# Two small products placed ahead of the last block of scores, and another engine that waits for the output

## The chip, the cores and the metric

The kernel runs on one core of one Trainium2 chip. The core has five engines with their own instruction streams: TensorE (PE, matrix products), VectorE (DVE), ScalarE (ACT), GpSimd (POOL) and SyncE (SP), which here issues nearly all transfers from device memory (HBM). The transfers are carried by 16 DMA engines. The engines meet only at semaphores. The metric is the device time of one execution in microseconds (us); less is better.

## The reference

One decode step of two blocks on the same input x (2 batches, 1 position, 1024 features), mixed by a gate. Only the parts that matter here:

```python
g = _sigmoid((x * gate_w).sum(-1, keepdims=True))
# a: attention with a cache, 32 heads of 128, 16384 cached positions, 2 batches
q = (x @ wq) by head
p = softmax(einsum("bhqd,bhkd->bhqk", q, k_cache) * 128 ** -0.5)
a = einsum("bhqk,bhkd->bhqd", p, v_cache) as rows @ wo
# b: a mixer and an MLP
h  = gelu(layernorm(x) @ w1)           # then shifted by +-1 and +-2 positions
x1 = x + shifted(h) @ w2               # one position only, so shifted(h) is zero
b  = x1 + gelu(layernorm(x1) @ w3) @ w4
return g * a + (1 - g) * b
```

All arrays are bf16. The two caches hold 268 MB each; with the weights 572.5 MB are read, once.

## The kernel before, in words

The attention is cut into 32 units: 16 pairs of heads times 2 batches (s = 0 and 1). A unit reads 8 MB of K and 8 MB of V. For a unit, SP loads K into one of two cells of SBUF (cell 0 for s = 0, cell 1 for s = 1). DVE turns it in 8 pieces into one of two buffers kt (L631, a transpose of 128 x 2048 words each), and PE computes the scores of a piece from it with 8 matmuls (L652, `pe_scores`). So there are 8 blocks of scores, and DVE's piece n waits for PE's block n - 2. After block 8, DVE transposes the scores (st, L636) and takes the maximum (m, L640); ACT makes a diagonal from it (Dm, L668), PE spreads it (R, L661), DVE takes the bound (nb, L688), ACT does the exponentials in two halves (L674), PE sums (tot, L697), and DVE takes the reciprocal (rinv, L693). The product with V (L702) follows in the unit's next turn, since the loop loads V of turn i - 1 in turn i. V has one cell, number 3.

The same cell 3 holds at first the big weights, one after the other: wq, then w3 (7 MB), then w4 (7 MB), then the first V. `linear` (L500) computes a row product such as x @ w3 with many small matmuls on PE (L510): 64 of 448 columns for w3, into the banks `oacc`, and 112 of 256 columns for w4, into the bank `ot`. `Line` (L21) notes which engine read and wrote what, and puts in the waits; `ln.dma` issues a load on SP after those who used the cell.

The first two units (s = 0, 1 of pair 0) are written out ahead of the loop by `first_unit` (L790). Around them the program text gives the order on each engine:

- SP: loads of wq, w1, w2, K of unit 0, then (when wq's product is done) w3, then K of unit 1 (L808, after DVE's piece 4 of unit 0), then w4 (L813, issued through L82, after w3's product), then the loop.
- PE: unit 0's 8 blocks, R and tot; then w3's product; then unit 1's 8 blocks, R and tot; then w4's product. Only then PE raises `pvd1` and `wod` (L828, L829).
- DVE: unit 0's pieces and softmax steps; then the transpose of w3's result (L816) and, together with ACT, the gelu that ends with h2T (L496); then unit 1's; then the rows `brow` (L834).

In the loop (L847, turns 1 to 15) SP waits and loads in this order: K for s = 0 (after DVE's piece 4 of s = 1 of the turn before), V of the turn before for s = 0 (L856, waits on `pvd1`), a piece of wo (L859, waits on `wod`), then K for s = 1 and V for s = 1. For the first turn `pvd1` is the increment of L828, so the first V waits for w4's product, because it overwrites w4's cell.

At the end, the two rows of the output go out from SP and ACT (L955), and SP waits for both landings (L959, L960), then all engines meet at the closing barrier.

Of the kernel before, what the change touches and what calls it, by code (L numbers as in the profile page):

```python
# [88 lines left out]
def kernel(  # L89
# [17 lines left out]
    B, Sq, D = A_x.shape  # L107
    _, H, Sk, Dh = A_k_cache.shape
    F = B_w3.shape[1]
    assert Sq == 1 and B == 2 and Dh == P and P == 128  # L110
    KC = D // P
    FC = F // P
# [6 lines left out]
    NCK = NJ // CT  # L119
# [13 lines left out]
    def sb(shape, dtype, name):  # L133
        return const.tile(shape, dtype, name=name)
# [3 lines left out]
    def S(name):  # L138
        if name not in sems:
            sems[name] = tc.alloc_semaphore(name)  # L140
        return sems[name]
# [5 lines left out]
    st = sb([P, GT, QP], FP32, "st")  # L147
# [26 lines left out]
    xn2T = sb([P, KC, B], BF16, "xn2T")  # L174
    h2T = sb([P, FC, B], BF16, "h2T")
# [19 lines left out]
    oacc = [oacc2[:, k, :] for k in range(2)]  # L195
# [4 lines left out]
    ot_ps = psum.tile([P, NQ], FP32, name="ot")  # L200

    def region(cell, elements):
        return mem[:, cell * CELL : cell * CELL + elements]
# [21 lines left out]
    def wait(engine, name, value):  # L225
        if isinstance(value, int) and value == 0:
            return
        engine.wait_ge(S(name), value)
# [7 lines left out]
    with tc.tile_critical(no_gpsimd_drain=True):  # L236
        PE, DVE, ACT, POOL, SP = nc.tensor, nc.vector, nc.scalar, nc.gpsimd, nc.sync
# [94 lines left out]
        def many(count, make, reads, writes):  # L332

            ln.wait("PE", ln.needs(reads, writes))
            for n in range(count):
                ins = make(n)
            stamp = ln._stamp(ins, "PE")
            ln.note(stamp, reads, writes)
            return stamp
# [160 lines left out]
        def linear(actT, w, R, N, act_key, w_key, banks, out_keys):  # L500

            G = N // Q4
            width = G // len(banks)
            jobs = [
                (r, g, k) for r in range(R) for k in range(len(banks)) for g in range(Q4)
            ]

            def one(n):
                r, g, k = jobs[n]
                return PE.matmul(  # L510
                    banks[k][QP * g : QP * g + B, 0:width],
                    lhsT=actT[:, r, :],
                    rhs=w[:, r, g * G + k * width : g * G + (k + 1) * width],
                    start=(r == 0),
                    stop=(r == R - 1),
                    skip_group_check=True,
                )

            return many(len(jobs), one, [act_key, w_key], out_keys)
# [85 lines left out]
        def chunk_ids(s):  # L605
            low, high = list(range(NCK // 2)), list(range(NCK // 2, NCK))
            return high + low if K_CELL[s] == 0 else low + high
# [4 lines left out]
        def pool_unit(i, s, hi):  # L612
            wait(POOL, f"sc{s}7", i)
            dst = qw[s][:, :, NG - 1 : NG - 1 + QP * (Q4 - 1) + 1 : QP]
            row = qd[:, i, s, :] if isinstance(i, int) else qd[:, bass.ds(i, 1), s, :].rearrange("p o v -> p (o v)")
            POOL.tensor_tensor(  # L616
                out=dst,
                in0=row.unsqueeze(2).to_broadcast([P, 4, Q4]),
                in1=mask4[:].unsqueeze(1).to_broadcast([P, 4, Q4]),
                op=ALU.mult,  # L620
            ).then_inc(S(f"qwd{s}"), 1)

        def dve_scores(i, s, hi, hi16):
            for n, c in enumerate(chunk_ids(s)):
                if n == 0:
                    wait(DVE, f"kl{s}", hi16)
                if n >= 2:
                    wait(DVE, f"sc{s}{n - 2}", hi)
                else:
                    wait(DVE, f"sc{1 - s}{n + 6}", hi if s else i)  # L630
                DVE.transpose(  # L631
                    out=kt[n % 2][:],
                    in_=k_view(s)[:, c * CT : (c + 1) * CT, :].rearrange("p j d -> p (j d)").bitcast(FP32),
                ).then_inc(S(f"tr{s}{n}"), 1)
            wait(DVE, f"sc{s}7", hi)
            DVE.transpose(  # L636
                out=st[:].rearrange("p j r -> p (j r)"), in_=sps[s][:]
            ).then_inc(S(f"stT{s}"), 1)
            wait(DVE, f"stT{s}", hi)
            DVE.tensor_reduce(out=m_t[:], in_=st[:, :, 0:NG], axis=AX.XY, op=ALU.max).then_inc(S(f"mx{s}"), 1)  # L640

        def pe_scores(i, s, hi):
            wait(PE, f"qwd{s}", hi)
            wait(PE, f"stT{s}", i)
            for n, c in enumerate(chunk_ids(s)):
                wait(PE, f"tr{s}{n}", hi)
                ktb = kt[n % 2][:].bitcast(BF16).rearrange("p (j w k e) -> p j w k e", j=CT, w=2, k=QP, e=2)
                for half in range(CT // GT):
                    m = c * (CT // GT) + half
                    for v in range(4):  # L650
                        w, e = divmod(v, 2)
                        ins = PE.matmul(  # L652
                            sps[s][:].rearrange("p (j k) -> p j k", k=QP),
                            lhsT=qw[s][:, v, NG - 1 - m : NG - 1 - m + P],
                            rhs=ktb[:, half * GT : (half + 1) * GT, w, :, e],
                            start=(n == 0 and half == 0 and v == 0),
                            stop=(n == NCK - 1 and half == CT // GT - 1 and v == 3),
                        )
                ins.then_inc(S(f"sc{s}{n}"), 1)
            wait(PE, f"dm{s}", hi)  # L660
            PE.matmul(R_ps[:, 0:P], lhsT=ones_f[:], rhs=Dm[:], start=True, stop=True).then_inc(S(f"rr{s}"), 1)  # L661

# [3 lines left out]
        def act_unit(i, s, hi):  # L666
            wait(ACT, f"mx{s}", hi)
            ACT.activation(out=Dm[:], in_=ident_s[:], func=ACTF.Copy, scale=m_t[:, 0:1]).then_inc(S(f"dm{s}"), 1)  # L668
            wait(ACT, f"nbd{s}", hi)
            if not (isinstance(i, int) and i == 0):  # L670
                wait(ACT, f"pvd{s}", pv_count(s, i, hi))
            for e in range(2):
                rows = slice(e * HALF, (e + 1) * HALF)
                ins = ACT.activation(  # L674
                    out=pts[s][rows, :, e, :].rearrange("p (m a) k -> p a k m", a=GT // 4),
                    in_=st[rows, :, 0:NG].rearrange("p (a k) m -> p a k m", k=4),
                    func=ACTF.Exp,
                    bias=nb_t[rows],
                    scale=scale,
                    accum_out=rs_t[rows],  # L680
                )
            ins.then_inc(S(f"ex{s}"), 1)

        def dve_nb(i, s, hi):
            wait(DVE, f"rr{s}", hi)
            for e in range(2):
                rows = slice(e * HALF, (e + 1) * HALF)
                ins = DVE.tensor_reduce(out=nb_t[rows], in_=R_ps[rows, rows], axis=AX.X, op=ALU.min)  # L688
            ins.then_inc(S(f"nbd{s}"), 1)
# [97 lines left out]
                )  # L787
            ins.then_inc(S(f"OTd{s}"), 1)

        def first_unit(s):  # L790
            if s == 0:
                for key in ("qd", "mask4", "qw0", "qw1"):
                    ln.wait("POOL", [ln.writer[key]])
            pool_unit(0, s, 1)
            if s == 0:
                ln.wait("ACT", [ln.writer["ident_s"], ln.writer["pt0"], ln.writer["pt1"]])
                ln.wait("PE", [ln.writer["lmat"], ln.writer["hsel"]])
            dve_scores(0, s, 1, 16)
            pe_scores(0, s, 1)
            act_unit(0, s, 1)  # L800
            dve_nb(0, s, 1)
            pe_tot(0, s, 1)
            dve_recip(0, s, 1)

        first_unit(0)
        wait(SP, "tr03", 1)
        ln.wait("SP", ln.needs([], ["w1", "w2"]))
        SP.dma_start(out=region(1, NJ * Dh), in_=unit_rows(k_rows, 0, 1)).then_inc(S("kl1"), 16)  # L808

        w3_v = region(3, KC * F).rearrange("p (r n) -> p r n", n=F)  # L810
        half = FQ // 2
        linear(xn2T, w3_v, KC, F, "xn2T", "c3", [oacc[0], oacc[1]], ["oacc0", "oacc1"])
        ln.dma("SP", region(3, FC * D), w_rows[3], "l_w4", writes=["c3"])  # L813
        ln.op(
            "DVE",
# [5 lines left out]
        )  # L821
        gelu_T(columns(FC), h2T[:], FC, "g2", "h2T")

        first_unit(1)
        w4_v = region(3, FC * D).rearrange("p (r n) -> p r n", n=D)
        linear(h2T, w4_v, FC, D, "h2T", "c3", [ot_ps[:]], ["ot"])
        ln.wait("PE", [ln.writer["ot"]])
        PE.sem_inc(S("pvd1"), 1)  # L828
        PE.sem_inc(S("wod"), 1)  # L829
# [17 lines left out]
        with nc.Fori(1, HP) as i:  # L847
            hi = nc.snap(i + 1)
# [104 lines left out]
        for b, queue in ((0, SP), (1, ACT)):  # L953
# [2 lines left out]
                out=out[b, 0].rearrange("(k n) -> k n", k=Q4),  # L956
                in_=out_row[b : b + QP * (Q4 - 1) + 1 : QP, :],
            ).then_inc(S(f"st{b}"), 16)
        for b, queue in ((0, SP), (1, SP)):  # L959
            wait(queue, f"st{b}", 16)  # L960


# [28 lines left out]
```

## Time and profile before

| what | value |
|---|---|
| median of 3 runs | 1337.51 us (1336.78 to 1337.55) |
| the profiled execution's own time | 1336.87 us |
| its span, first to last instruction | 1335.1 us |
| mean granted TensorE clock | 0.805 of full |
| PE, DVE, ACT, POOL busy | 752.2, 710.4, 104.6, 12.4 us |
| read from HBM | 572.53 MB, 429 GB/s over the span |
| SP's transfer queue (q1) | 99.4% of the time of 16 engines |
| K load, median from issue to landing | 28.2 us |
| w3's product on PE | 82.38 us, for 6.00 us |
| w4's product on PE | 118.77 us, for 4.90 us |

How to read it: the profile is one execution, recorded by the chip. The page lists busy time by engine, the transfer queues, the chain of work that ended last, and groups of instructions by source line (L652 is line 652). The timeline lists start, duration, engine, line, operation, and in brackets the idle time before it and who ended that. "PEclk" is the share of TensorE's full clock that was granted. "Landing" is when a transfer's semaphore shows that all of it has arrived.

### The profile page before, as it was taken

What the parts mean: (1) busy time and instruction counts of PE and PEld (TensorE: products, weight loads), DVE (VectorE), ACT (ScalarE), POOL (GpSimd) and SP (SyncE); (2) the same over time, 40 slices, a digit from 0 to 9 for tenths busy, and PEclk for the clock granted to TensorE, in tenths of its full rate; (3) what the DMA queues carried; (4) which work ended last, traced back from release to release, by engine and by line L of the source; (5) the groups of instructions that cost most, each with busy time, mean ns of one, the idle gap of its engine ahead of it and who ended that gap; (6) DMA issues with size and microseconds to landing.
All of it is one profiled execution on the core that took longest, in us unless ns stands there. A gap on an engine that the chain in (4) does not pass through costs nothing.

```text
span 1335.1 us, 11620 instructions
## 1 busy us (share of the span) xinstructions
PE 752.2 (56%) x4920; PEld 302.5 (23%) x4920; DVE 710.4 (53%) x712; ACT 104.6 (8%) x164; POOL 12.4 (1%) x44
## 2 busy tenths in 40 slices
PE   0665666554566555466655546655455665555664
PEld 0222222222222222222222212222222222222222
DVE  1555565654556654456565445656444656545561
ACT  0010000000000000000000000000000000000000
POOL 0000000000000000000000000000000000000000
PEclk9778887777888777788777788877778887777886
DMA  9999999999999999999999999999999999999997
GB/s 409 437 393 429 450 425 440 432 423 444 428 438 428 438 432 426 442 426 440 428 438 434 424 442 424 442 428 435 436 424 442 424 444 426 430 442 424 442 424 327
DMA packets 13993, 572.68 MB, mean 429 GB/s; under 512 B 1936, under 2 KB 1952, under 8 KB 4384
## 3 DMA queue, kind: packets, MB, share of 16 engines
q1 hardware_dynamic: 13544, 572.53, 99.4%
q8 instruction: 8, 0.13, 0.0%
q10 hardware_dynamic: 440, 0.01, 0.0%
q14 instruction: 1, 0.01, 0.0%
HBM read 572.53 MB, written 0.00 MB: 429 GB/s over the span
## 4 chain that ended last, share of the span: by engine, by line
DMA 68%; DVE 17%; PE 12%; issue 2%; SPq 0%; ACT 0%; POOL 0%; ACTq 0%; POOLq 0%
DMA mem<-in_A_k_cache_dram 64%; DVE kt L631 16%; PE S L652 11%; DMA gwT<-in_gate_w_dram 2%; DMA mem<-in_A_v_cache_dram 2%; PE oacc L510 1%; PE oacc L702 0%; SPq L879 0%; ACT pt L674 0%; SPq L854 0%; DVE st L636 0%; POOL ln_rstd L450 0%; PE tot L344 0%; DVE tsc L527 0%; DVE tsc L816 0%
## 5 line engine op out<-in xcount | busy, mean ns | idle before, releaser
L652 PE MATMUL S<-kt,qw 128*128 128x512 bf16 x2048 | 547.5, 416 | 303.0 <-DVE kt L631 302.6
L631 DVE STREAM_TRANSPOSE kt<-mem 128x2048 f32<-128x2048 f32 x256 | 570.4, 2282 | 205.0 <-DMA mem<-in_A_k_cache_dram 153.2
L652 PEld LDWEIGHTS S<-kt,qw 128*128 128x128 bf16 x2048 | 195.3, 104 | 642.8 <-issue 335.4
L702 PE MATMUL oacc<-mem,pt 128*8 128x512 bf16 x2008 | 117.3, 387 | 3.9 <-DMA mem<-in_A_v_cache_dram 3.9
L674 ACT ACTIVATE pt<-st,nb 64x256 bf16<-64x256 f32 x64 | 89.7, 1401 | 226.0 <-DVE nb L688 225.5
L750 DVE TENSOR_SCALAR part<-oacc,maskr 128x128 f32<-128x128 f32 x31 | 10.9, 351 | 143.0 <-PE oacc L702 143.0
L668 ACT ACTIVATE Dm<-ident_s,m 128x128 f32<-128x128 f32 x32 | 12.8, 401 | 917.6 <-DVE m L640 917.6
L697 PE MATMUL tot<-rs,lmat 128*128 128x1 f32 x64 | 18.7, 362 | 105.4 <-ACT pt L674 105.4
L693 DVE RECIPROCAL rinv<-tot 128x1 f32<-128x1 f32 x32 | 5.4, 169 | 113.1 <-PE tot L697 113.1
L702 PEld LDWEIGHTS oacc<-mem,pt 128*8 128x8 bf16 x2008 | 46.4, 88 | 61.9 <-issue 4.2
L636 DVE STREAM_TRANSPOSE st<-S 128x512 f32<-128x512 f32 x32 | 23.0, 718 | 64.2 <-PE S L652 64.2
L719 PE MATMUL ot<-hsel,red 128*128 128x2 f32 x120 | 19.0, 263 | 54.7 <-DVE red L756 54.7
L661 PE MATMUL R<-Dm,ones_f 128*128 128x128 f32 x64 | 15.6, 326 | 54.4 <-ACT Dm L668 54.4
L697 PEld LDWEIGHTS tot<-rs,lmat 128*128 128x128 f32 x64 | 16.0, 310 | 112.3 <-ACT pt L674 112.3
L719 PEld LDWEIGHTS ot<-hsel,red 128*128 128x128 f32 x120 | 16.4, 196 | 69.8 <-DVE red L756 69.8
L674 ACT ACTIVATION_READ_ACCUMULATOR pt<-st,nb 64x1 f32 x64 | 30.6, 478 | 0.0
L661 PEld LDWEIGHTS R<-Dm,ones_f 128*128 128x128 f32 x64 | 9.5, 188 | 70.2 <-ACT Dm L668 70.2
L756 DVE SCALAR_TENSOR_TENSOR part<-oacc,maskr,part 128x128 f32<-128x128 f32 x62 | 21.7, 351 | 2.2
L784 DVE CAST OT<-ot 64x2 bf16<-64x2 f32 x60 | 9.6, 160 | 22.2 <-PE ot L719 21.8
L344 PE MATMUL tot<-zp,ones_f 128*128 128x2 f32 x2 | 0.6, 363 | 33.4 <-DVE zp L366 33.4
L616 POOL TENSOR_TENSOR qw<-qd,mask 128x16 bf16<-128x16 f32 (+1 forms) x32 | 8.3, 263 | 1150.3 <-PE S L652 1150.3
L688 DVE TENSOR_REDUCE nb<-R 64x1 f32<-64x64 f32 x64 | 14.2, 222 | 3.4 <-PE R L661 2.1
(104 smaller groups left out, 120.1 us busy)
## 6 DMA issues: line engine op xcount, KB each, us to landing
mem<-in_B_w_dram SPq DMA_DIRECT2D x2, 7168.0 KB, 25.5
wo<-in_A_wo_dram SPq DMA_DIRECT2D x15, 512.0 KB, 28.5
mem<-in_A_v_cache_dram SPq DMA_DIRECT2D x7, 1024.0 KB, 20.3
mem<-in_B_w_dram SPq DMA_DIRECT2D x2, 2048.0 KB, 29.0
mem<-in_A_v_cache_dram SPq DMA_DIRECT2D x2, 512.0 KB, 27.6
mem<-in_A_k_cache_dram SPq DMA_DIRECT2D x32, 28.2
wo_last<-in_A_wo_dram SPq DMA_DIRECT2D x2, 256.0 KB, 21.6
mem<-in_A_v_cache_dram SPq DMA_DIRECT2D x31, 30.9
```

Of the source, the lines that this page charges most:

```text
L510: return PE.matmul(banks[k][QP * g : QP * g + B, 0:width], lhsT=actT[:, r, :], rhs=w[:, r, g * G + k * width : g * G + (k + 1) * width], s ...
L631: DVE.transpose(out=kt[n % 2][:], in_=k_view(s)[:, c * CT : (c + 1) * CT, :].rearrange("p j d -> p (j d)").bitcast(FP32),).then_inc(S(f"tr ...
L636: DVE.transpose(out=st[:].rearrange("p j r -> p (j r)"), in_=sps[s][:]).then_inc(S(f"stT{s}"), 1)
L652: ins = PE.matmul(sps[s][:].rearrange("p (j k) -> p j k", k=QP), lhsT=qw[s][:, v, NG - 1 - m : NG - 1 - m + P], rhs=ktb[:, half * GT : (ha ...
L661: PE.matmul(R_ps[:, 0:P], lhsT=ones_f[:], rhs=Dm[:], start=True, stop=True).then_inc(S(f"rr{s}"), 1)
L668: ACT.activation(out=Dm[:], in_=ident_s[:], func=ACTF.Copy, scale=m_t[:, 0:1]).then_inc(S(f"dm{s}"), 1)
L674: ins = ACT.activation(out=pts[s][rows, :, e, :].rearrange("p (m a) k -> p a k m", a=GT // 4), in_=st[rows, :, 0:NG].rearrange("p (a k) m ...
L688: ins = DVE.tensor_reduce(out=nb_t[rows], in_=R_ps[rows, rows], axis=AX.X, op=ALU.min)
L697: PE.matmul(tot_ps[:, 0:1], lhsT=lmat[:], rhs=rs_t[:], start=True, stop=True).then_inc(S(f"tt{s}"), 1)
L702: ins = PE.matmul(oacc[s][QP * q : QP * q + 8, :], lhsT=pts[s][:, g].rearrange("p h k -> p (h k)"), rhs=V[:, 4 * g : 4 * g + 4, :].rearran ...
L719: ins = PE.matmul(ot_ps[:, 2 * r : 2 * r + 2], lhsT=red[:].rearrange("p e d -> p (e d)")[:, r : 2 * Dh : 2], rhs=hsel[:], start=True, stop ...
L756: ins = DVE.scalar_tensor_tensor(out=red[:] if twice else part[:], in0=in0.unsqueeze(1).to_broadcast([P, 2, Dh]) if twice else in0, scalar ...
```

## The change

`pe_scores` takes a function `between` and calls it after block 7 of the 8. `first_unit` passes it on. For unit 0 the function is w3's product, for unit 1 it is w4's; both were calls behind `first_unit` before. On PE the order becomes: blocks 1 to 7, the product, block 8, R, tot. The order on DVE, ACT and SP, the transfers and the two increments behind `first_unit(1)` stay as they are. At the end GpSimd waits for the two landings in place of SP.

```diff
-        def pe_scores(i, s, hi):
+        def pe_scores(i, s, hi, between=None):
...
                 ins.then_inc(S(f"sc{s}{n}"), 1)
+                if between is not None and n == NCK - 2:
+                    between()
...
-        def first_unit(s):
+        def first_unit(s, between):
...
-            pe_scores(0, s, 1)
+            pe_scores(0, s, 1, between)
...
-        first_unit(0)
+        w3_v = region(3, KC * F).rearrange("p (r n) -> p r n", n=F)
+        w4_v = region(3, FC * D).rearrange("p (r n) -> p r n", n=D)
+        banks = [oacc[0], oacc[1]]
+        first_unit(0, lambda: linear(xn2T, w3_v, KC, F, "xn2T", "c3", banks, ["oacc0", "oacc1"]))
         wait(SP, "tr03", 1)
         ln.wait("SP", ln.needs([], ["w1", "w2"]))
         SP.dma_start(out=region(1, NJ * Dh), in_=unit_rows(k_rows, 0, 1)).then_inc(S("kl1"), 16)
...
-        linear(xn2T, w3_v, KC, F, "xn2T", "c3", [oacc[0], oacc[1]], ["oacc0", "oacc1"])
         ln.dma("SP", region(3, FC * D), w_rows[3], "l_w4", writes=["c3"])
...
-        first_unit(1)
-        w4_v = region(3, FC * D).rearrange("p (r n) -> p r n", n=D)
-        linear(h2T, w4_v, FC, D, "h2T", "c3", [ot_ps[:]], ["ot"])
+        first_unit(1, lambda: linear(h2T, w4_v, FC, D, "h2T", "c3", [ot_ps[:]], ["ot"]))
         ln.wait("PE", [ln.writer["ot"]])
         PE.sem_inc(S("pvd1"), 1)
         PE.sem_inc(S("wod"), 1)
...
-        for b, queue in ((0, SP), (1, SP)):
-            wait(queue, f"st{b}", 16)
+        for b in range(B):
+            wait(POOL, f"st{b}", 16)
```

More of the change, by code (lines that the diff above doesn't have):

```diff
@@ L808 @@
         SP.dma_start(out=region(1, NJ * Dh), in_=unit_rows(k_rows, 0, 1)).then_inc(S("kl1"), 16)
-        w3_v = region(3, KC * F).rearrange("p (r n) -> p r n", n=F)
         half = FQ // 2
-        linear(xn2T, w3_v, KC, F, "xn2T", "c3", [oacc[0], oacc[1]], ["oacc0", "oacc1"])
         ln.dma("SP", region(3, FC * D), w_rows[3], "l_w4", writes=["c3"])
```

## The prediction

> **What bounds the kernel now.** I read the page first: span, transfer queues, chain.
>
> ```profile
> span 1335.1 us, 11620 instructions
> DMA  9999999999999999999999999999999999999997
> q1 hardware_dynamic: 13544, 572.53, 99.4%
> q8 instruction: 8, 0.13, 0.0%
> DMA 68%; DVE 17%; PE 12%; issue 2%; SPq 0%; ACT 0%; POOL 0%; ACTq 0%; POOLq 0%
> ```
>
> The 16 DMA engines are busy in every slice. SP's queue q1 holds 99.4% of their time, and the chain that ended last is mostly K transfers. So only two things can be gained: stretches in which the transfer engines stand still, and the tail after the last bytes. Next I read SP's issues in order of time (start us, duration us):
>
> ```profile
> 39.12 0.33 SPq L82 DMA_DIRECT2D mem<-in_B_w_dram  x1
> 65.50 0.33 SPq L808 DMA_DIRECT2D mem<-in_A_k_cache_dram  x1
> 88.49 0.33 SPq L82 DMA_DIRECT2D mem<-in_B_w_dram  x1
> 102.11 0.35 SPq L854 DMA_DIRECT2D mem<-in_A_k_cache_dram  x1
> 123.97 0.34 SPq L856 DMA_DIRECT2D mem<-in_A_v_cache_dram  x1
> ```
>
> These are w3, K of unit 1 (call it k01), w4, K of loop turn 1 (k10), and the first V (v00). The transfer view of the narrow windows around them gives, in its last column, the time from issue to landing:
>
> ```profile
> mem<-in_B_w_dram SPq DMA_DIRECT2D x1, 7168.0 KB, 31.3
> mem<-in_A_k_cache_dram SPq DMA_DIRECT2D x1, 24.4
> mem<-in_B_w_dram SPq DMA_DIRECT2D x1, 7168.0 KB, 19.6
> ```
>
> w3 lands at 39.1 + 31.3 = 70.4, k01 at 65.5 + 24.4 = 89.9, w4 at 88.5 + 19.6 = 108.1. w4 was issued only 1.4 us before the queue ahead of it ran out. The transfer view of 86 to 92 us (40 slices of 0.15 us, each packet counted where it starts) shows the hole:
>
> ```profile
> DMA  0900909000000000000000099999009000000000
> ```
>
> No packet starts between 87.05 and 89.45 us. In the full queue each engine starts one every 2.4 us (64 KB). The trace's packet records (start, duration, bytes; no engine number) put it more finely. The last 16 packets of k01 end at 87.53 to 88.11 on 13 engines and at 88.67, 89.35 and 89.48 on three. The first 16 of w4 start at 89.44 to 90.56 and take 2.79 us on average; the next 16, of the same size, take 2.12 to 2.13. The packets show no other hole of all engines after it; a row of the stretches view (last two columns: transfer share, GB/s) agrees:
>
> ```profile
> 125.00:1290.00 1165.00, 670.57 (x4114) 265.94 (x4115) 645.87 (x591) 93.04 (x145) 7.37 (x28) 0.81 1.00 433
> ```
>
> What makes w4 late is this stretch of the timeline:
>
> ```profile
> 74.30 1.91 PE L652 MATMUL S<-kt,qw 128*128 128x512 bf16 x8 [0.29 <-DVE kt L631]
> 81.86 0.59 PE L697 MATMUL tot<-rs,lmat 128*128 128x1 f32 x2 [3.41 <-ACT pt L674]
> 82.38 6.00 PE L510 MATMUL oacc<-mem,xn2T 128*2 128x448 bf16 x64
> 88.44 1.12 DVE L816 STREAM_TRANSPOSE tsc<-oacc 128x896 f32<-128x896 f32 x1 [5.78 <-PE oacc L510]
> 118.77 4.90 PE L510 MATMUL ot<-mem,h2T 128*2 128x256 bf16 x112
> ```
>
> w3's product waits in PE's order behind unit 0's whole softmax, though w3 landed at 70.4; SP's w4 load waits for the product, since w4 goes into the same cells.
>
> **Part 1, w3's product.** It moves ahead of 8 score matmuls, R (L661) and tot (L697). Block 7 of the scores ends at 72.11 + 1.91 = 74.0, 3.6 us after w3 landed, so no new wait. Its 64 matmuls took 6.0 us at the granted clock 0.50 (slices 82 to 88); at 74 us the clock is 1.00. The nearest warm row is wq's product, whose last 32 matmuls of 512 columns ran from 36.87 to 39.04, 0.068 us each: 64 x 0.068 x 448/512 = 3.8 us. Bounds 3.8 and 6.0; I take 3.8, the same clock. It ends at 77.8, and w4 is issued at about 77.9 instead of 88.5, 9 us before k01's last packets. The hole goes.
>
> What is late instead: the last block, and with it the transpose L636, m, Dm, R, nb, exp and tot, go back by 3.8 us (tot ends at 86.3 instead of 82.45). DVE's transpose L816 no longer waits 5.8 us, so h2T is ready at about 86.4 + 2.84 = 89.3 instead of 91.3 (91.5 with the cold 6.0 us). k01 lands at 89.9, so unit 1's transposes start at 89.9 instead of 91.19. None of this is on the transfers' path unless an issue comes late. k10 went out 10.9 us after those transposes began: now 100.8 (102.4 cold), with w4 in flight until 104.5 on the fastest engine. From issue to first packet took 88.49 to 89.44, 0.95 us, so k10 must go out by 103.5: covered by 1.1 to 2.7 us.
>
> Worth of the hole: without it w4's eight packets per engine (8 x 2.118 = 16.94 us) follow k01's at once. The fast engines then end at 87.53 + 16.94 = 104.47 instead of 106.88, a gain of 2.41; the slowest at 89.48 + 16.94 = 106.42 instead of 107.77, a gain of 1.35. Landing differences say the same as the lower figure: w4 18.2 us after k01, w3 by packets 16.9. Which counts? Each engine keeps its lag to the end, and the end waits for the one furthest behind. The six fetches of instructions on q8 before 300 us (49.1, 85.5, 122.1, 136.3, 176.2, 278.8 us) and one on q14 (55.7) each put one engine 1.0 to 1.5 us back; the hole let the engines hit before 88 us catch up. Those hit later end 2.26 us behind the fastest, at 1308.6 against 1306.34 in the last whole V load. Without the hole the early laggards keep 1.14, 1.82 and 1.95. If other engines are hit later (0 to 0.58 + 1.45, about 2.0), the end gains 2.41 + 2.26 - 2.0 = 2.6; if an early laggard is hit again (lag 3.3), 2.41 + 2.26 - 3.3 = 1.3. The q8 fetches seem to fall on different engines within each stretch (lags of 1.14, 1.82, 1.95 before the hole; 1.61, 1.88, 1.91, 2.26 after it, none near 3), so I take 2.5 and keep 1.3.
>
> The Trainium skill ("Runtime: NRT & Kernel Launch", Instruction fetch mechanics) says that programs are refilled in 16 KiB blocks and that the cost is mostly hidden. The blocks agree (8 packets, 0.13 MB); by "hidden" there would be no lags and the gain would be 2.4 flat, but the packet rows show 1.0 to 1.5 us taken from one engine each time.
>
> **Part 2, w4's product.** It moves ahead of unit 1's last block. Block 7 now ends at 89.9 + 19.3 (before: 91.19 to 110.47) = 109.2; w4 lands at 106.9, covered by 2.3 us. Its 112 matmuls at the warm rate (56 in 1.67 us in slice 122 to 124, clock 0.94) take 3.3 us, cold 4.9. Then the last block, 1.9 us, and from its end to tot's end 6.2 us as before: 120.8. SP waits on PE's increment of pvd1, which still stands behind tot: v00 goes out at 120.9 (cold, and with h2T late too, up to 123.8) instead of 123.97. The fastest engine now finishes k10 at 123.8 (126.23 less 2.41), so v00 must go out by 122.9: covered by 2.0 us. In the old order it would go out at 123.97 - 1.3 = 122.7, also in time by 0.2 us. So this part is worth 0 by itself; it is cover for Part 1.
>
> **Part 3, POOL waits for the output.** POOL has nothing behind those waits but the closing barrier; SP reaches it early. SP saw the landings at 1332.8 and 1333.15 and the span ended at 1335.1. One hop from SP to POOL falls away (POOL moved 0.20 us after SP's release), but POOL wakes later: its qw L616 began 0.18 us after its releaser, DVE's st on the same one after 0.02. Bounds -0.2 and +0.2; I take 0, as both rows are alike.
>
> **Sum.** -2.5 (bounds -1.3, and -2.7 when no lag exceeds 1.95) + 0 + 0 (bounds -0.2 and +0.2). The profiled execution took 1336.87 (span 1335.1 and 1.8 around it): 1334.4. The median of the runs, 1337.51, lies 0.64 above it: 1335.0.
>
> **Rivals.**
> - Partial gain: a later fetch hits an engine that is already behind. For it: nothing ties a fetch to a fast engine. Against: no double lag so far. Gain 1.0 to 2.1, time 1335.4 to 1336.5, say 1336.2.
> - The transfers are hidden anyway (no gain): if idle engines only mirror a limit of memory. Against: 433 GB/s everywhere else, and the hole is empty. 1337.5.
> - Larger gain: the bound 2.7, the 0.2 of the tail and up to 0.4 because the order of the engines at the end changes under the two fetches of the tail (1325.2, 1328.9 us): 2.7 to 3.3, say 3.1, time 1334.4. For it: before, the last engine was one of four hit late. Against: all terms must fall well.
> - Slower: the hole moves to v00. The inserted w4 product, if cold and if h2T is late too, pushes tot, pvd1 and v00's issue past 122.9. Every us past it costs one; beyond 125.4 the gain is gone, beyond 128.1 it is 0.2% slower, 1340.2. For it: pvd1 still waits for exp, and v00 feeds everything after. Against: even 123.8 costs 0.9 us only.
>
> The Trainium skill ("DMA: Bandwidth & Descriptors", Why a DMA increments its semaphore by 16 and not by 1) has the engines finish independently and the semaphore count all sixteen; the spread of k01's ends (1.95 us) agrees. By it a landing shows only the last engine, so 1.35 would be the floor of the worth and not its size.
>
> **Chances.** 0.2% is 2.7 us, about what a measurement can tell from no change. Full gain (2.2 to 2.7) 0.52, partial 0.20, larger 0.18, none 0.05, slower 0.05. The full case ends at the line, and the runs scatter by 0.4 either way: 0.22 of its 0.52 I put beyond it. Faster 0.22 + 0.18 = 0.40, same 0.55, slower 0.05. Range: the partial case's far end plus 0.3 for the scatter of the runs (1336.78 to 1337.55) gives 1336.8; the larger gain gives 1334.2.
>
> **What the profile after would show.** w4 issued near 78 us, no empty stretch at 87 to 89.5, k10 landing at 126.3 to 127.6 instead of 128.8, v00 issued before 122.9, every loop issue earlier by 1.3 to 2.6 us, the w3 product near 3.8 us, POOL named as waiting for the output. Wrong would be: a new stretch without packet starts near 104 or 124 us, or one engine 3 us behind at 1300 us.

## The result, and the profile after

The changed kernel takes 1335.08 us (median of 15 runs, 1334.19 to 1337.31); beside it the kernel before takes 1337.67 (15 runs, 1336.53 to 1339.77). The ratio is 0.998, 95% interval 0.9972 to 0.9988: 2.6 us less, with a range of 1.6 to 3.7. The profiled execution took 1336.28 us, more than most of its runs (five of the 15 lie between 1334.19 and 1334.35). Its trace shows why, and that turned out to be the larger lesson.

The page of the changed kernel, the lines that answer to those of before:

```profile
span 1334.5 us, 11620 instructions
...
DMA  9999999999999999999999999999999999999997
...
q1 hardware_dynamic: 13544, 572.53, 99.4%
q8 instruction: 8, 0.13, 0.0%
...
DMA 70%; DVE 15%; PE 12%; issue 1%; SPq 0%; POOL 0%; ACTq 0%; ACT 0%; POOLq 0%
```

The kernel is bound as before. SP's issues in order of time (start us, duration us):

```profile
40.13 0.33 SPq L82 DMA_DIRECT2D mem<-in_B_w_dram  x1
66.57 0.33 SPq L813 DMA_DIRECT2D mem<-in_A_k_cache_dram  x1
78.31 0.33 SPq L82 DMA_DIRECT2D mem<-in_B_w_dram  x1
101.51 0.35 SPq L855 DMA_DIRECT2D mem<-in_A_k_cache_dram  x1
120.69 0.34 SPq L857 DMA_DIRECT2D mem<-in_A_v_cache_dram  x1
```

w4 goes out at 78.3 instead of 88.5 us and the first V (v00) at 120.7 instead of 124.0. But w3 and K of unit 1 (k01), which no edit touches, go out 1.0 and 1.1 us later than in the trace of before. The timeline of the moved products and of their surroundings:

```profile
73.18 1.91 PE L652 MATMUL S<-kt,qw 128*128 128x512 bf16 x8 [0.28 <-DVE kt L631]
...
75.02 3.20 PE L510 MATMUL oacc<-mem,xn2T 128*2 128x448 bf16 x64
...
78.15 1.91 PE L652 MATMUL S<-kt,qw 128*128 128x512 bf16 x8
...
85.72 0.59 PE L699 MATMUL tot<-rs,lmat 128*128 128x1 f32 x2 [3.41 <-ACT pt L676]
...
86.43 1.10 DVE L819 STREAM_TRANSPOSE tsc<-oacc 128x896 f32<-128x896 f32 x1
...
109.79 3.23 PE L510 MATMUL ot<-mem,h2T 128*2 128x256 bf16 x112
```

Both products run between blocks 7 and 8 with no wait in front and at a granted clock of 1.00 (in the trace of before it was 0.50 for w3's, and 0.50 and then 0.94 for w4's): 3.20 us instead of 6.00, 3.23 instead of 4.90. The transfer view of 86 to 92 us:

```profile
DMA  9000000909999909900000080989899000000809
```

Packets start through 87.05 to 89.45 us, where none did before. The packet records agree: k01's last 16 packets end at 87.98 to 90.37 us, w4's first 16 start at 87.98 to 90.23. What is new stands one transfer earlier. The transfer view of 65 to 73 us (slices of 0.2 us), of the kernel before:

```profile
DMA  6006099960060067997007000700999007000700
```

and of the changed kernel:

```profile
DMA  0606669900006067997000999099999000000988
```

The first has starts near 68.2 to 70.0 us and then its steady rhythm; in the second they are strewn from 68.0 to 71.2. By the packet records, paired by ends and starts, five engines start k01 0.8 to 1.5 us late. Two words are used for this from here on. The lead of a transfer is the time from its issue to the moment at which the first of the 16 engines has finished the packets queued ahead of it. Its loss is the mean over the 16 engines of the time that they stand still at its start, plus what the first packet takes beyond its usual time. k01 lost 0.71 us here. Its lead was only 1.50 us (issued at 66.57, first engine through with w3 at 68.07); before, it was 2.68 us (65.50, 68.18), with no loss. The cause of that lies still earlier: wq's product on TensorE took 6.27 us here and 5.08 in the trace of before, the same 64 matmuls. This trace is called the disturbed one below. So the two profiled executions differ by more than the change, and their spans, 0.6 us apart, are not its size.

### The profile page after: what moved, and what is told of

It is laid out like the page before. It is cut to its first block, busy times and chain, and to the rows that moved or that the text cites. A ratio compares the mean times of both kernels' runs of the same rounds, so it can differ in the third digit from the quotient of the medians.

```text
span 1334.5 us, 11620 instructions
## 1 busy us (share of the span) xinstructions
PE 748.2 (56%) x4920; PEld 302.0 (23%) x4920; DVE 710.5 (53%) x712; ACT 104.6 (8%) x164; POOL 12.3 (1%) x44
## 4 chain that ended last, share of the span: by engine, by line
DMA 70%; DVE 15%; PE 12%; issue 1%; SPq 0%; POOL 0%; ACTq 0%; ACT 0%; POOLq 0%
DMA mem<-in_A_k_cache_dram 66%; DVE kt L631 15%; PE S L652 11%; DMA gwT<-in_gate_w_dram 2%; DMA mem<-in_A_v_cache_dram 2%; PE oacc L510 0%; PE oacc L704 0%; SPq L880 0%; SPq L855 0%; PE tot L344 0%; POOL ln_rstd L450 0%; DVE tsc L527 0%; PE arow L946 0%; DVE st L636 0%; PE R L934 0%
## 5 line engine op out<-in xcount | busy, mean ns | idle before, releaser
L752 DVE TENSOR_SCALAR part<-oacc,maskr 128x128 f32<-128x128 f32 x31 | 10.9, 351 | 141.8 <-PE oacc L704 141.8
```

What stands on the lines that cost most here:

```text
L752: ins = DVE.tensor_scalar(out=part[:], in0=in0, scalar1=mask[:, 0:1], scalar2=None, op0=ALU.mult)
```

## The experiments

The first four separate the parts and lengthen the hole. Each is compared with the kernel before on its own chip (1338.21 us, 33 runs).

**w3's product alone.** As the change, but `first_unit(1)` without a product in it, w4's product behind it as before, and SP waits.

```diff
-        first_unit(1, lambda: linear(h2T, w4_v, FC, D, "h2T", "c3", [ot_ps[:]], ["ot"]))
+        first_unit(1, None)
+        linear(h2T, w4_v, FC, D, "h2T", "c3", [ot_ps[:]], ["ot"])
```

> The hole theory: the time falls because w4's load is issued before the transfer queue has run empty, and only w3's place does that. So this part alone gives the change's gain less the shorter end: 2.2 to 2.5 us faster than before, w4 issued near 78 us, no stretch without packet starts at 87 to 89.5 us, v00 issued near 123 us without a new hole. The v00 rival (the gain comes from the earlier first V): within 0.4 us of before.

Measured: 1336.86 us (11 runs, 1335.42 to 1338.52), ratio 0.9993, interval 0.9984 to 1.0002. The median is 1.35 us down where 2.2 to 2.5 were expected. SP's issues in its trace:

```profile
66.75 0.33 SPq L813 DMA_DIRECT2D mem<-in_A_k_cache_dram  x1
78.50 0.33 SPq L82 DMA_DIRECT2D mem<-in_B_w_dram  x1
103.76 0.36 SPq L856 DMA_DIRECT2D mem<-in_A_k_cache_dram  x1
125.67 0.34 SPq L858 DMA_DIRECT2D mem<-in_A_v_cache_dram  x1
```

w4 is early and its hole is gone. But the first engine finished w4 at 105.44 us and K of the loop's first turn (k10) at about 125.7, so k10 and v00 were issued with leads of 1.7 and 0.1 us or less and lost 0.67 and 1.23 us: the hole came back at v00. k01, too, had lost 1.02 us, at a lead of 1.35. The profiled execution was the slowest of the 11 runs (1338.52), so these losses are more than is usual. The hole theory was right for w4 and wrong in "v00 without a new hole".

**w4's product alone.** The converse: `first_unit(0, None)`, w3's product behind it, w4's between blocks 7 and 8 of unit 1, and SP waits.

> The hole theory: w4 is still issued near 88.5 us, the hole at 87 to 89.5 us stays, and v00, issued near 122 us instead of 124, was covered before: no change, within 0.4 us. The v00 rival: 2 us faster.

Measured: 1337.18 us (1336.28 to 1338.04), ratio 0.9995, interval 0.9986 to 1.0004: not told from no change. w4 was issued at 88.75 us and lost 2.65 us; v00 at 121.61, without loss. So w4's product alone leaves the first hole where it was, and the v00 rival's 2 us are excluded (the interval ends at 1.9 us faster).

**GpSimd waits, nothing else.**

> From the two traces the end, from the second landing of the output to the last instruction, is 1.94 us with SP waiting and 1.68 us with GpSimd: 0.27 us faster, at the edge of what can be told. A rival that gives the end the whole gain: 2 us or more faster.

Measured: 1337.29 us (1336.46 to 1338.58), ratio 0.9998, interval 0.9988 to 1.0007. The times alone can't tell 0.27 us from none here; they exclude 2 us. The 0.27 stands on the two traces: from the branch behind the second landing to the last instruction 1333.15 to 1335.10 us with SP, 1332.83 to 1334.51 with GpSimd. In the second, most of the other engines' closing steps and of SP's own are done before the landing. This run's own trace has 1.67 us for the same stretch.

This trace also shows how much the hole of the old order varies, though nothing ahead of the end was edited:

```profile
82.65 4.52 PE L510 MATMUL oacc<-mem,xn2T 128*2 128x448 bf16 x64
...
87.27 0.33 SPq L82 DMA_DIRECT2D mem<-in_B_w_dram  x1
```

w3's product took 4.52 us here, 6.00 in the trace of before and 6.10 with w4's product alone (the granted clock was 0.50 all through the two long ones, and 1.00 again by 86 us in this one). w4 then lost 0.84, 2.31 and 2.65 us.

**A longer hole.** The kernel before, with SP held until h2T is ready:

```diff
-        ln.dma("SP", region(3, FC * D), w_rows[3], "l_w4", writes=["c3"])
...
         gelu_T(columns(FC), h2T[:], FC, "g2", "h2T")
+        ln.wait("SP", [ln.writer["h2T"]])
+        ln.dma("SP", region(3, FC * D), w_rows[3], "l_w4", writes=["c3"])
```

> The order of before, but SP holds w4's load back until h2T is ready, near 91.3 us instead of 88.5: 2.8 us. The hole theory: every engine stands 2.8 us longer and nothing gives it back, so 2.8 us slower (2.3 to 3.2). The rival that the transfers are hidden anyway: no change.

Measured: 1339.67 us (1338.34 to 1340.33), ratio 1.0014, interval 1.0005 to 1.0023: 1.5 us slower by the medians. w4 went out at 91.13 us, 2.64 us later than in the trace of before. The transfers are not hidden; the rival falls. That 2.6 us cost only 1.5 has a reading: k01 lost 0.70 us in this trace, and the long hole lets late engines catch up, so such losses no longer add, while they do add in most runs of before. The two traces alone differ by 2.9 us (spans 1338.0 and 1335.1). Against the least disturbed runs of before (the lowest ten of the 33: 1336.65 to 1337.28) it is 2.4 to 3.0 slower. This reading was not tested by itself.

What these four left open was why k01, k10 and v00 lost time although their issues came 0.1 to 2.3 us ahead of the first idle engine, and why runs of one kernel differ by 3 us. The theory I formed: an issue needs a lead of about 2.5 us over the first engine that runs dry (lead theory), and the length of wq's product moves those leads from run to run. The next runs put 14 idle matmuls ahead of the gate, so that wq's product no longer follows a long idle stretch of TensorE (a warm start; without it a start is called cold). In the cold traces its matmuls run at a slow pace first, eight in 0.85 us, and at eight in 0.43 us later: from about the 28th matmul on in the trace of before, from about the 51st in the disturbed one. The clock row reads 1.00 for both and doesn't show this. The idle matmuls compute nothing that is used.

```diff
+        many(
+            14,
+            lambda n: PE.matmul(
+                sps[0][:], lhsT=rep4[:, 0, :], rhs=rep4[:].rearrange("p g m -> p (g m)"),
+                start=True, stop=True, skip_group_check=True,
+            ),
+            ["rep4", "xT"], ["warm"],
+        )
         compute_gate()
```

**The warm start on the kernel before.**

> The kernel before with 14 idle products on TensorE ahead of the gate, so that wq's product runs at the full clock and its length (5.0 to 6.3 us so far) no longer moves the issues that follow. Lead theory: what a late issue costs goes by its lead over the first engine that runs dry, and a lead under 2.5 us already costs. Then K of unit 1 goes out 1 to 2 us earlier with a lead of 3 us or more and loses nothing, w4 goes out 1 to 2 us earlier (near 87 us) and its hole shrinks from 2.3 us to 1 or less: 1.0 to 2.0 us faster than before. Rival (the scatter comes from elsewhere): no change in the median and the same scatter of 3 us.

**On w3's product alone.**

> The warm start and w3's product early, w4's product in its old place, SP waits at the end. Lead theory: no loss at K of unit 1 and at w4; the first V goes out near 122.5 us with a lead of about 1.5 us and loses 0.5 to 0.9 us, which w4's early product would save. 2.0 to 2.6 us faster than before. Rival (w4's product is worth nothing): equal to the next kernel within 0.3 us beyond the 0.27 of the end.

**On the changed kernel.**

> The changed kernel with the warm start. Lead theory: no loss at any of the first issues; 1334.3 us or less, 0.5 to 1.0 us faster than the changed kernel's median and 3.2 to 3.8 us faster than before, with a scatter below 1.5 us. Rival: as the changed kernel, 2.5 us faster than before.

**On w4's product alone** (run later, with the delayed V's below).

> The kernel before with the warm start and w4's product early, w3's in its old place. Lead theory: w4 goes out near 86.2 us with a lead of 1.2 us and loses 0.3 to 0.8 us, the first V is on time (it lost 0.9 us in the old place): 0.5 to 1.0 us faster than the warm kernel before (1336.35). Rival (w4's product is worth nothing): as the warm kernel before.

In all four traces wq's product takes 3.6 us, at the fast pace from its start, and k01 goes out 3.3 us or more ahead and loses nothing. The leads and losses of w4 and v00 by the packet records, in us, and the time:

| warm start and | w4 lead, loss | v00 lead, loss | median (range) us | ratio, interval |
|---|---|---|---|---|
| kernel before | 1.22, 0.33 | 0.53, 0.93 | 1336.35 (1335.32 to 1338.52) | 0.999, 0.9981 to 0.9999 |
| w3 early | 11.1, 0.01 | 0.24, 1.03 | 1335.48 (1334.66 to 1336.91) | 0.9984, 0.9975 to 0.9993 |
| w4 early | 0.64, 0.92 | 5.1, 0.00 | 1335.90 (1335.01 to 1336.63) | 0.9984, 0.9975 to 0.9993 |
| the whole change | 10.9, 0.01 | 3.85, 0.00 | 1334.24 (1334.04 to 1334.35) | 0.9974, 0.9964 to 0.9985 |

The first three have a short lead somewhere, and scatter over 1.6 to 3.2 us; the last has none, and its eight runs lie within 0.31 us. w4's early product on top of w3's is worth 1.24 us less the 0.27 of the end, about 1.0; all runs of the one lie below all runs of the other even with 0.27 added. The rival "w4's product is worth nothing" falls. The transfer view of 121 to 129 us (slices of 0.2 us) shows v00's start, with w3 early only:

```profile
DMA  0799700070970000099090970000000009990000
```

and with the whole change:

```profile
DMA  7099900007777099770007097099770007097099
```

In the second, the engines go on one after another. In the first, twelve engines are through with k10 at 123.7 to 124.2 us, none starts v00 before 124.46, and they start close to the late ones.

**An earlier k01 without the warm start.** The changed kernel, with the four additions into x1row (1.8 us of DVE ahead of unit 0's transposes) moved to where DVE waits for the exponentials:

```diff
-        for g in range(Q4):
-            rows = slice(QP * g, QP * g + B)
...
+        def add_x1row():
+            for g in range(Q4):
+                rows = slice(QP * g, QP * g + B)
...
         layernorm_T(x1T[:], xn2T[:], "ln2", "x1T", "xn2T")
...
             dve_nb(0, s, 1)
+            if s == 0:
+                add_x1row()
             pe_tot(0, s, 1)
```

> The changed kernel, cold start, with the four additions of x1row moved behind the bounds of unit 0, where VectorE stands still. The layer norm's chain ahead of unit 0 gets 1.8 us shorter, so K of unit 1 goes out 1.3 us earlier, at a lead of 2.5 us or more. Lead theory: its loss of 0 to 1.0 us goes, 0.3 to 0.8 us faster than the changed kernel, 3.0 to 3.4 faster than before. Rival: as the changed kernel.

Measured: 1334.14 us (9 runs, 1334.03 to 1335.02), ratio 0.9972, interval 0.9962 to 0.9982; its kernel before was 1338.06 (28 runs). SP's and DVE's lines in its trace:

```profile
40.23 0.33 SPq L82 DMA_DIRECT2D mem<-in_B_w_dram  x1
64.41 0.33 SPq L817 DMA_DIRECT2D mem<-in_A_k_cache_dram  x1
76.16 0.33 SPq L82 DMA_DIRECT2D mem<-in_B_w_dram  x1
...
80.67 1.78 DVE L599 TENSOR_TENSOR x1row<-ot,xrow 2x256 f32<-2x256 f32 x4
...
84.18 0.17 DVE L697 RECIPROCAL rinv<-tot 128x1 f32<-128x1 f32 x1 [1.73 <-PE tot L701]
```

wq's product took 6.25 us, as long as in the disturbed trace above, and w3 went out as late (40.2 us). Yet k01 left at 64.4 us, 3.64 us ahead of the first idle engine, and lost nothing. So the loss at k01 comes from its lead and not from the slow product as such. This is the best version found, 2.8 per mille under the kernel before, with no useless work in it. Every run but one lies within 0.32 us.

**The first V with a chosen lead.** The changed kernel with the warm start, and 2, 4 or 7 idle matmuls on TensorE between unit 1's tot and the release of v00:

```diff
         ln.wait("PE", [ln.writer["ot"]])
+        many(
+            2,
...
+            ["rep4"], ["warm"],
+        )
+        ln.wait("PE", [ln.writer["warm"]])
         PE.sem_inc(S("pvd1"), 1)
         PE.sem_inc(S("wod"), 1)
```

> The changed kernel with the warm start, and 2 idle products on TensorE between tot and the release of the first V, so that V goes out about 1.3 us later (near 121.2 us), 2.6 us ahead of the first engine that runs dry (123.8). Lead theory (a lead under 2.5 us costs): 0 to 0.2 us slower than the changed kernel with the warm start (1334.24). The rule of the prediction (0.95 us are enough): no loss.

> The same with 4 idle products: V goes out near 122.1 us, a lead of 1.7 us. Lead theory, from the losses seen at such leads in the other traces (0.5 to 0.7 us): 0.4 to 0.8 us slower than 1334.24. The rule of the prediction: no loss.

> The same with 7 idle products: V goes out near 123.4 us, a lead of 0.4 us. Lead theory: 0.9 to 1.5 us slower than 1334.24. The rule of the prediction: 0.5 us.

| idle matmuls | v00 issued | lead | mean loss per engine | median (range) us | ratio, interval |
|---|---|---|---|---|---|
| 0 | 119.97 | 3.85 | 0.00 | 1334.24 (1334.04 to 1334.35) | 0.9974, 0.9964 to 0.9985 |
| 2 | 121.59 | 2.09 | 0.31 | 1335.32 (1334.09 to 1335.70) | 0.9977, 0.9968 to 0.9986 |
| 4 | 122.12 | 1.70 | 0.63 | 1335.82 (1334.24 to 1336.92) | 0.9983, 0.9974 to 0.9992 |
| 7 | 123.68 | 0.16 | 1.26 | 1336.26 (1334.89 to 1337.40) | 0.9985, 0.9976 to 0.9994 |

The prediction's rule (an issue 0.95 us ahead is in time) gives 0, 0 and, at the lead of 0.16 us, 0.8. The lead theory is right in kind and too low in size: it expected at most 0.2, 0.8 and 1.5 us, and measured are 1.1, 1.6 and 2.0 us over the kernel without these idle matmuls, by the medians. That kernel ran on another chip; the kernel before took 1338.06 us there and 1338.19 here. At a lead of 2.09 the runs fall in two groups, four at 1334.09 to 1334.39 and seven at 1334.98 to 1335.70. The mean loss understates the time, since the end waits for the engine furthest behind: in the last whole V load the spread from the first engine's last packet to the last one's is 2.04 us with lead 3.85 and 3.26 with lead 2.09, in the traces.

## Why the prediction was right or wrong

The number and the range held: 1335.0 forecast, 1335.08 measured, and the full-gain case came. Part of that was luck: part 1 was priced too high and part 2 too low, and the two errors nearly cancel. The median also stands for runs of two kinds: five near 1334.25, and others up to 1337.31, of which the one that was traced had a short lead at k01.

- **What bounds the kernel, and the hole.** Right. The empty stretch at 87 to 89.5 us is gone when w4 is issued early and stays when it is not; lengthened, it costs time.
- **Part 1, the times.** w4's issue 77.9 forecast, 78.3 measured; tot's end 86.3 and 86.3; h2T 89.3 and 89.2; v00's issue 120.9 and 120.7; k10's 100.8 and 101.5. The moved product took 3.20 us, not 3.8. The row was misread: 36.87 us is the start of wq's last 32 weight loads; its last 32 matmuls start at 37.11, which gives 0.059 us each and 3.3 us. The loop's next issues came only 0.6 to 0.8 us earlier in the disturbed trace (K at 139.14 instead of 139.71), where 1.3 to 2.6 was forecast, and 2.5 us earlier in the changed kernel with the warm start (137.22).
- **Part 1, the worth.** 2.5 us was given to the w3 product alone. Alone it moved the median by 1.35 us (interval from 2.1 faster to 0.3 slower), and with the warm start by 0.87 (where w4's hole in the old order was only 0.33 us). The hole of the one execution that was read (2.31 us per engine) was read rightly, but it is not what the other runs have: 0.84 us in the trace with GpSimd's waits. And without part 2 some of it comes back at k10 and v00.
- **Part 2, "worth 0 by itself; it is cover for Part 1".** This step failed. It put v00 in the old place at 122.7 us, "in time by 0.2 us", from 0.95 us between issue and first packet. With w3's product alone early, v00 went out at 123.5 us (warm start) and 125.7. And the 0.95 us came from engines that were already idle; it is when the first of them starts. A queue that must not run dry needs more: at leads of 2.49 us and over 0.10 us or less was lost, at 1.70 us 0.63, at 0.24 us and less 1.0 to 1.3. Measured, part 2 is worth about 1.0 us on top of part 1.
- **Part 3, 0 within 0.2.** 0.27 us by the traces, a little outside. The hop from SP to GpSimd fell away, and most of the other engines' and of SP's closing steps moved ahead of the landing; I had counted the hop alone.
- **The lag of single engines.** The step that each engine keeps its lag to the end, and that the end waits for the last, holds: the last 4 KB packets of V end at 1328.49 us before, 1328.16 in the changed kernel's disturbed trace, 1326.07 and 1326.05 in the two without short leads, and the spans are 1335.1, 1334.5, 1332.4 and 1332.4. The two undisturbed traces end 2.04 and 2.10 us spread, near the 2.0 that the prediction took for fetches that fall on different engines. So no double hit was seen in them.
- **The rivals.** The partial gain did occur, in the profiled execution itself (1336.28 us), by the mechanism that the prediction named, a fetch that hits an engine already behind, and by one that it did not name. k01's short lead came first: by the packet records, eight engines finish w4 1.5 to 2.4 us behind the first, of which the three fetches until then account for three at most. Then the fetches at 112.0 and 136.0 us fall on engines 2.3 and 2.0 us behind, and these two finish v00 3.7 and 3.6 us behind the first (143.54). After the fetches at 175.9 and 276.1 us it is four engines, at 1307.95 to 1308.27 in the last whole V load against 1304.53 for the first. So a sign that the prediction gave for being wrong, one engine 3 us behind at 1300 us, came true in this execution. The larger gain came in the five runs near 1334.25, 3.4 us under the median of before and 2.3 under its lowest run. A hole at v00, the slower rival, is what part 2 prevents: it is real at a lead of 0.1 us or less, and never cost more than the gain.

All together, the transfers that had a short lead in the traces (lead in us; mean loss in us): 2.68: 0.01 (before, k01); 2.49: 0.10; 2.30: 0.34; 2.26: 0.01 (before, v00); 2.09: 0.31; 1.75: 0.70; 1.70: 0.63; 1.68: 0.67; 1.58: 0.51; 1.50: 0.71 (changed, k01); 1.35: 1.02; 1.22: 0.33; 0.64: 0.92; 0.53: 0.93; 0.42: 0.84; 0.24: 1.03; 0.16: 1.26; 0.1 or less: 1.23; issued after the first engine was idle by 0.96 us: 2.31 (before, w4), by 1.19: 2.65, by 2.93: 3.95. So the lead doesn't settle the loss alone (2.30 lost 0.34 and 2.26 lost 0.01, 1.22 lost 0.33 and 1.35 lost 1.02).

The Trainium skill ("DMA: Bandwidth & Descriptors", Specifications) gives about 0.6 us to the first byte for transfers issued from SP. The trace of before shows more: w4's first packet came 0.95 us after the issue, the last engine's first packet 2.07 us after it (88.49 to 90.56), and the first packets took 2.79 instead of 2.12 us on average. The 2.07 and the 0.67 make 2.7, near the 2.5 us of lead that cost nothing. Why a short lead also lengthens the first packet is not shown by these runs.

## What to carry to other kernels

Where the transfer queue is the bound, list each transfer's issue beside the moment at which the first engine finishes what is queued ahead of it; in this kernel leads under some 2.5 us cost time, though not each of them in each trace (1.1 us by the medians at a lead of 2.09, 2.0 at 0.16). The busy digits of the page read 9 all the same. Look at the whole chain of issues, since a hole that is closed at one transfer comes back at the next that has too short a lead. When runs of one kernel scatter more than those of a variant, look for a lead at the edge: here the scatter fell from 3 us to 0.3 with the warm start, and to 1.0 (0.3 without one run) with x1row's additions moved, once the last short lead was gone.

## What the runs showed of the hardware that was not expected

- The same 64 matmuls of wq took 5.08, 6.27 and 6.25 us in cold traces, with nothing changed in front of them, and 3.6 after idle matmuls. It counted only because the later issues hung on it, k01's above all. w3's product in its old place took 4.52 to 6.10 us, and w4's issue moved with it. How far the two account for the scatter of the runs is known only from the versions in which the leads are long; the runs without a trace have no such record.
- Each fetch of 16 KB of instructions takes one transfer engine for 1.0 to 1.1 us, and by the packet records the next packet of the engine that stood still takes 2.9 us instead of 2.42 (for example 112.96 us in the disturbed trace): about 1.45 us in all. The kernel waits for the last engine: 2.04 and 2.10 us behind the first in the two best traces. That these lags are the fetches' alone was read from the times, not tested. Why the fetches in the disturbed trace all fell on engines already behind, and in the two best traces none did, is not shown.
- The best two versions agree to 0.1 us by different means, 1334.24 and 1334.14: with no lead under 2.5 us, what is left, by their traces, is the transfers' own time, the lag of single engines, and the 6.3 us from V's last packet to the last instruction.
